# One shared SBUF arena and one PSUM block against many separate tiles, in a state-space and long-convolution kernel

## The chip, the core and the metric

The kernel runs on one NeuronCore of a Trainium2 chip. The core has five engines with an instruction queue each: TensorE (PE, matmuls; PEld are its weight loads), VectorE (DVE), ScalarE (ACT), GpSimd (POOL) and SyncE (SP, which here only issues DMAs). Each queue runs strictly in its written order; engines wait for one another, and for DMAs, through semaphores. The metric is device time in microseconds (us) of one execution.

## What is computed

Two sequence mixers read the same `x` (2048 steps, 1024 channels) and are blended by a gate of one number per step. Cut to what matters:

```python
x = A_x
g = sigmoid((x * gate_w).sum(-1, keepdims=True))
# a: complex diagonal state space model, 1024 states
h = Lam_bar[None, :] * h + Bu[:, t, :]          # for each of the 2048 steps
y = 2.0 * einsum("blp,dp->bld", hseq, Cmat).real + x * Dskip
# b: 4-tap shift convolution of k, times v, then a 2048-long convolution per channel by FFT
kv = k_shift * v
y = irfft(rfft(kv_pad) * rfft(kf_pad))[:S] + kv * ssm_D
b = x * y
return g * a + (1 - g) * b
```

## The kernel before

**Two halves in one program.** The convolution `b` is done in 8 units of 128 channels (`for u in range(NU)`). A unit loads `k` and `v` transposed (L522, L523, DMA transposes on SP), makes the short convolution by matmuls (L558) and multiplies by `v` (DVE, L561), stores the product to DRAM (L568, POOL) and loads it back in another layout together with the filter (L573, POOL, one load each). Then come the matrix form of the FFT: `stage1` (matmul L589; its results are copied from PSUM into the place `z`), `spec` (matmuls L602 to L604, copied into `kv`), `product` (DVE, L614 to L617, into `pp`), `inverse` (matmuls L628 to L630, copied into `qq`), and four DMAs of 64 KB from `qq` into `zb` (L635, on SP; 4 for each of 4 quarters of a unit, 128 in all). `zb` is laid out by partitions, and each of these DMAs writes every sixteenth partition, beginning with partition `k2`. `final` (matmuls L648, L649) reads `zb`, and its result goes to DRAM (L652).

The state space half `a` goes by 4 blocks of 512 steps. For each of 8 groups of states, `rot_ops` makes a rotation table (DVE L709 to L711 in F32 in the places `wt1` and `wt2`, then ACT L714 and L305), `in_ops` multiplies (matmul L742), rotates (DVE L752 to L754), scans (L757) and rotates back (L766 to L768). `c_ops` prepares the output matrices (L799, L803), and `out_ops` multiplies by them (matmuls L825, L831), gates (ACT L835), adds (DVE L837) and stores (L838). The first block's groups are interleaved with the 8 convolution units; the second, third and fourth blocks fill what is left and the end.

**Copies out of PSUM** all go through one helper, `evac`: ACT does it on L426, DVE on L424, whichever a planner chose. 172 of the 1024-column copies are ACT's, 36 are DVE's.

**What sets the order.** `Planner` lists every operation, gives each buffer a place by number and each operation an engine and a slot, and the program is written out in that order; a chain of order-only edges at the end keeps every engine's instructions in it. `places` gives the permitted numbers for each kind of buffer, in KB of a partition for SBUF ("S") and in banks for PSUM ("P"): `z` lies at 80 to 95, `zb` at 96 to 103 or 188 to 195, `wt1` at 164 and 165, `wt2` at 166 and 167, `qq` at 120 and 121 or 122 and 123. `view` turns a place into an address: in this kernel a slice of one SBUF tile `arena` or of one PSUM tile `banks`. The semaphore waits are put in afterwards by the recording layer, which compares each instruction's accesses with earlier accesses to the same tile.

Of the kernel before, what the change touches and what calls it, by code (L numbers as in the profile page):

```python
# [11 lines left out]
BF16 = mybir.dt.bfloat16  # L12
F32 = mybir.dt.float32
# [162 lines left out]
def kernel(  # L176
# [25 lines left out]
    S, D = xf.shape  # L202
# [17 lines left out]
    consts = ctx.enter_context(tc.tile_pool(name="consts", bufs=1))  # L220
    dram = ctx.enter_context(tc.tile_pool(name="dramscr", bufs=1, space=bass.MemoryType.DRAM))
    parm = ctx.enter_context(tc.tile_pool(name="parm", bufs=1))
    psum = ctx.enter_context(tc.tile_pool(name="psum", bufs=1, space=bass.MemoryType.PSUM))
    pB_scr = dram.tile([S, D], BF16, name="pB_scr")
    kv_scr = dram.tile([D, S], BF16, name="kv_scr")
    pB_v = pB_scr.rearrange("(j g) d -> j g d", g=16)
    AR_KB = 201
    arena = consts.tile([128, AR_KB * 512], BF16, name="arena")
    banks = psum.tile([128, 8, 512], F32, name="banks")


    def at(first, n, step, *guards):
        return [(first + step * i, guards) for i in range(n)]
# [7 lines left out]
    if 1 == 2:  # L241
# [18 lines left out]
        "ot": ("S", 2, free2 + extra),  # L260
        "ps": ("P", 2, at(0, 4, 2)), "bu": ("P", 2, at(6, 1, 0) + at(0, 3, 2)), "psy": ("P", 2, at(0, 4, 2)),
    }
    pl = Planner(places)
    pl.limit = {"ps": 4, "bu": 2, "psy": 3, "x": 4, "pb": 4, "ga": 3, "ot": 4, "cs": 8}
    op = pl.op

    def view(t):
        mem, size, _ = places[t.tag]
        dims = t.shape[1:]
        n = math.prod(dims)  # L270
        if mem == "P":
            flat = banks[:, t.off:t.off + size, :].rearrange("p a b -> p (a b)")
            if t.dt is BF16:
                flat = flat.bitcast(BF16)
            flat = flat[:, 0:n]
        elif t.dt is F32:
            flat = arena[:, t.off * 512:t.off * 512 + 2 * n].bitcast(F32)
        else:
            flat = arena[:, t.off * 512:t.off * 512 + n]
        if len(dims) == 1:  # L280
            return flat
        names = "abcdef"[:len(dims)]
        return flat.rearrange(f"p ({' '.join(names)}) -> p {' '.join(names)}", **dict(zip(names, dims)))

    T.look = staticmethod(view)
    PE, ACTE, DVE, POOL = "PE", "ACT", "DVE", "POOL"
    MM = {512: 0.216, 256: 0.112, 128: 0.064}
# [296 lines left out]
    def stage1(a, z, w, q):  # L584
        ps = tile_("ps", [128, 4, 256], F32)

        def f(e):
            for i in range(4):
                nc.tensor.matmul(ps.ap[:, i, :], lhsT=a.ap[:, 4 * q + i, :], rhs=tabS.ap[:, 0:256], start=True, stop=True)  # L589
        o = op({PE: 4 * MM[256]}, f, [a, rT1], [ps, z])  # L590
        evac(lambda: z.ap[:, :, w, :, 32 * q:32 * q + 32].rearrange("p k r (g c) -> p k r g c", c=8),
             lambda: ps.ap.rearrange("p g (k r c) -> p k r g c", r=2, c=8), [ps], [z], 1.05)
        return o
# [48 lines left out]
    def final(zb, u, h):  # L642
        ps, cv = tile_("ps", [128, 2, 4, CH], F32), tile_("cv", [128, 8, CH])

        def f(e):
            for i in range(2):
                g0 = 8 * h + 4 * i
                nc.tensor.matmul(ps.ap[:, i], lhsT=tabS.ap[:, 256:384], rhs=zb.ap[:, g0:g0 + 4, 0, :], start=True, stop=False)  # L648
                nc.tensor.matmul(ps.ap[:, i], lhsT=tabS.ap[:, 384:512], rhs=zb.ap[:, g0:g0 + 4, 1, :], start=False, stop=True)  # L649
        o = op({PE: 4 * MM[512]}, f, [zb, rT2], [ps, cv])  # L650
        evac(lambda: cv.ap, lambda: ps.ap.rearrange("p a g c -> p (a g) c"), [ps], [cv])
        op(dma("POOL", 256), lambda e: nc.gpsimd.dma_start(  # L652
            out=pB_v[:, 8 * h:8 * h + 8, u * CH:(u + 1) * CH], in_=cv.ap), [cv], [convd])
        return o

    for u in range(NU):
# [8 lines left out]
        for q in range(4):  # L665
            pl.key = base + 0.5 * q - 4.0
            o = stage1(kas[u], zz[u], 0, q)
# [17 lines left out]
        for h in range(2):  # L685
            o = final(zb, u, h)
# [221 lines left out]
```

## Time and profile before

| | |
|---|---|
| time before, median of 2 runs | 595.6 us (593.55 to 597.65) |
| the profiled execution's own time | 594.96 us |
| its span, first to last instruction | 593.2 us |
| PE busy | 432.5 us, 73% |
| DVE busy | 383.4 us, 65% |
| ACT busy | 290.0 us, 49% |
| POOL busy | 62.1 us, 10% |

The share of busy time is a mean over very different stretches, so the table by stretches and the lists of waits say more. "Granted clock" is the share of TensorE's full speed (2.4 GHz; the lower of its two levels is 1.2 GHz) that the records show. Idle time before an instruction stands in square brackets in a timeline, with what ended it; "issue" there means that no releaser was found. "SPq" is a DMA issue on SP's queue.

### The profile page before, as it was taken

How to read it: one execution, taken by the hardware profiler on the slowest of the kernel's cores; microseconds unless marked ns; L12 is line 12 of the kernel's file. 1: busy time of each engine (PE TensorE's matmuls, PEld its weight loads, DVE VectorE, ACT ScalarE, POOL GpSimd, SP SyncE). 2: the span in 40 equal slices, each digit the busy share in tenths (PEclk: the TensorE clock that was granted, in tenths of full speed). 3: DMA queues.
4: the chain of work that ended last, by engine and by line, in shares of the span. 5: the costliest groups of instructions: out<-in, count | busy, mean ns of one | idle time of the engine just before them, and what ended most of it. 6: DMA issues, size and time to landing. Idle time of an engine off the chain costs nothing. (4 is left out here: it accounts for less than half of the span.)

```text
span 593.2 us, 6880 instructions
## 1 busy us (share of the span) xinstructions
PE 432.5 (73%) x2529; PEld 235.2 (40%) x2529; DVE 383.4 (65%) x573; ACT 290.0 (49%) x364; POOL 62.1 (10%) x102
## 2 busy tenths in 40 slices
PE   2527755945836765914764684796999999999996
PEld 1424333532524442512342352452444445444443
DVE  6567680933834645602657381698999999998950
ACT  5685424733734545512644562697895223322111
POOL 3210010100010010102011010000211102000000
PEclk9778785987977787875896796798999999999999
DMA  7899583462731732466242331375852446100100
GB/s 132 184 191 207 123 134 73 117 111 53 152 88 40 142 94 63 88 130 146 62 134 65 69 88 36 71 148 119 184 137 71 143 90 179 52 19 18 38 35 36
DMA packets 118026, 60.25 MB, mean 102 GB/s; under 512 B 93416, under 2 KB 109800, under 8 KB 117992
## 3 DMA queue, kind: packets, MB, share of 16 engines
q1 hardware_dynamic: 109576, 34.62, 29.9%
q0 software_dynamic: 7296, 25.17, 16.2%
q8 instruction: 20, 0.33, 0.2%
q10 hardware_dynamic: 1120, 0.02, 0.1%
q14 instruction: 14, 0.11, 0.1%
HBM read 16.80 MB, written 12.58 MB: 50 GB/s over the span
## 5 line engine op out<-in xcount | busy, mean ns | idle before, releaser
L426 ACT CAST arena<-banks 128x1024 bf16<-128x1024 f32 x172 | 165.9, 1019 | 190.7 <-DMA arena<-arena 100.9
L742 PE MATMUL banks<-arena 128*128 128x512 bf16 x512 | 124.0, 394 | 9.9 <-ACT arena L426 5.8
L825 PE MATMUL banks<-arena 128*128 128x512 bf16 x512 | 117.4, 381 | 1.3 <-DVE arena L803 1.1
L589 PE MATMUL banks<-arena 128*128 128x256 bf16 x256 | 43.1, 324 | 60.3 <-ACT arena L426 57.2
L742 PEld LDWEIGHTS <-arena 128*128 128x128 bf16 x512 | 51.4, 101 | 69.8 <-issue 17.8
L825 PEld LDWEIGHTS <-arena 128*128 128x128 bf16 x512 | 49.5, 98 | 59.2 <-issue 2.5
L602 PE MATMUL banks<-arena 128*128 128x512 bf16 x128 | 53.3, 416 | 24.9 <-ACT arena L426 17.3
L424 DVE CAST arena<-banks 128x1024 bf16<-128x1024 f32 x36 | 43.4, 1220 | 28.8 <-DMA arena<-arena 17.2
L589 PEld LDWEIGHTS <-arena 128*128 128x128 bf16 x256 | 28.7, 113 | 71.9 <-issue 64.2
L628 PE MATMUL banks<-arena 128*128 128x256 bf16 x128 | 33.4, 293 | 19.7 <-DVE arena L424 9.0
L835 ACT ACTIVATE arena<-banks,gcols 128x1024 bf16<-128x1024 f32 x16 | 17.5, 1113 | 46.1 <-PE banks L825 46.0
L558 PE MATMUL banks<-arena 128*128 128x512 bf16 (+1 forms) x112 | 34.4, 468 | 7.5 <-DMA arena<-in_B_k_dram 3.3
L614 DVE TENSOR_TENSOR arena<-arena 128x1024 bf16<-128x1024 bf16 x32 | 21.9, 684 | 26.3 <-ACT arena L426 26.2
L603 PE MATMUL banks<-arena 128*128 128x256 bf16 x128 | 37.5, 293 | 0.0
L604 PE MATMUL banks<-arena 128*128 128x256 bf16 x128 | 37.4, 292 | 0.0
L652 POOL DMA_DIRECT2D pB_scr<-arena x16 | 14.3, 893 | 163.8 <-ACT arena L426 156.6
L630 PE MATMUL banks<-arena 128*128 128x128 bf16 x128 | 29.9, 233 | 0.0
L629 PE MATMUL banks<-arena 128*128 128x128 bf16 x128 | 29.9, 233 | 0.0
L752 DVE TENSOR_TENSOR arena<-arena 128x1024 bf16<-128x1024 bf16 x32 | 21.9, 685 | 11.3 <-ACT arena L305 10.8
L648 PE MATMUL banks<-arena 128*128 128x512 bf16 x32 | 13.0, 407 | 18.3 <-ACT arena L426 6.6
L837 DVE TENSOR_TENSOR arena<-arena 128x1024 bf16<-128x1024 bf16 x16 | 11.0, 688 | 22.9 <-ACT arena L835 22.8
L709 DVE TENSOR_SCALAR arena<-iota_row,thn 128x512 f32<-128x512 f32 x8 | 3.9, 485 | 33.5 <-DMA arena<-arena 19.8
(162 smaller groups left out, 631.1 us busy)
## 6 DMA issues: line engine op xcount, KB each, us to landing
arena<-arena SPq DMA_DIRECT2D x128, 64.0 KB
arena<-in_B_ssm_k_dram POOLq DMA_DIRECT2D x8, 512.0 KB, 6.0
kv_scr<-arena POOLq DMA_DIRECT2D x8, 512.0 KB, 4.4
arena<-kv_scr POOLq DMA_DIRECT2D x8, 512.0 KB, 6.0
pB_scr<-arena POOLq DMA_DIRECT2D x16, 256.0 KB, 3.6
arena<-in_A_x_dram POOLq DMA_DIRECT2D x16, 256.0 KB, 3.5
arena<-pB_scr POOLq DMA_DIRECT2D x16, 256.0 KB, 4.0
out_dram<-arena SPq DMA_DIRECT2D x16, 256.0 KB
```

The source lines that it names most:

```text
L424: nc.vector.tensor_copy(o(), i_())
L426: nc.scalar.copy(o(), i_())
L558: nc.tensor.matmul(ps.ap[:, i, lo:512], lhsT=dg.ap[:, s_, :], rhs=kT.ap[:, t0 + lo - s_:t0 + 512 - s_], start=(s_ == 0), stop=(s_ == KS - 1))
L589: nc.tensor.matmul(ps.ap[:, i, :], lhsT=a.ap[:, 4 * q + i, :], rhs=tabS.ap[:, 0:256], start=True, stop=True)
L602: nc.tensor.matmul(o, lhsT=tabF.ap[:, 0, k2, :], rhs=x, start=True, stop=False)
L603: nc.tensor.matmul(o[:, :, 0, :], lhsT=tabF.ap[:, 1, k2, :], rhs=x[:, :, 1, :], start=False, stop=False)
L604: nc.tensor.matmul(o[:, :, 1, :], lhsT=tabF.ap[:, 2, k2, :], rhs=x[:, :, 0, :], start=False, stop=True)
L628: nc.tensor.matmul(o, lhsT=tabG.ap[:, 0, k2, :], rhs=x, start=True, stop=False)
L629: nc.tensor.matmul(o[:, 0, :], lhsT=tabG.ap[:, 2, k2, :], rhs=x[:, 1, :], start=False, stop=False)
L630: nc.tensor.matmul(o[:, 1, :], lhsT=tabG.ap[:, 1, k2, :], rhs=x[:, 0, :], start=False, stop=True)
L742: nc.tensor.matmul(ps.ap[:, r, :], lhsT=BT[dt_][r].ap[:, pi * 128:(pi + 1) * 128], rhs=xT.ap[:, dt_, :], start=(dt_ == 0), stop=(dt_ == ND ...
L825: nc.tensor.matmul(psy.ap[:, dh, :], lhsT=hbs[(tb, pi)].ap[:, r, tl * 128:(tl + 1) * 128], rhs=CT[pi][r].ap[:, dh * 512:(dh + 1) * 512], s ...
```

## The change

`arena` is replaced by a list of tiles: the SBUF places of all kinds of buffers are sorted, those that overlap are joined into a span, and every span gets a tile of its own (57 of them, `ar0`, `ar1`, ...). `z` and each place of `zb`, `qq`, `wt1`, `wt2`, `kv` and so on thereby lie in tiles of their own. `banks` becomes four tiles of two banks each. `view` looks up the tile of a place. Shapes, types and the planner's tables are as they were. Line numbers behind the new lines are 9 higher.

```diff
-    AR_KB = 201
-    arena = consts.tile([128, AR_KB * 512], BF16, name="arena")
-    banks = psum.tile([128, 8, 512], F32, name="banks")
+    banks = [psum.tile([128, 1024], F32, name=f"bank{i}") for i in range(4)]
...
+    spans = []
+    for a, b in sorted((o, o + size) for m, size, offs in places.values() if m == "S" for o, _ in offs):
+        if spans and a < spans[-1][1]:
+            spans[-1][1] = max(b, spans[-1][1])
+        else:
+            spans.append([a, b])
+    home = {}
+    for i, (a, b) in enumerate(spans):
+        t = consts.tile([128, (b - a) * 512], BF16, name=f"ar{i}")
+        for k in range(a, b):
+            home[k] = (t, a)
...
         if mem == "P":
-            flat = banks[:, t.off:t.off + size, :].rearrange("p a b -> p (a b)")
+            flat = banks[t.off // 2]
             if t.dt is BF16:
                 flat = flat.bitcast(BF16)
             flat = flat[:, 0:n]
-        elif t.dt is F32:
-            flat = arena[:, t.off * 512:t.off * 512 + 2 * n].bitcast(F32)
         else:
-            flat = arena[:, t.off * 512:t.off * 512 + n]
+            a, a0 = home[t.off]
+            a0 = (t.off - a0) * 512
+            flat = a[:, a0:a0 + 2 * n].bitcast(F32) if t.dt is F32 else a[:, a0:a0 + n]
```

In the built programs each engine has the same instructions in the same order before and after; what differs is what they wait for. In the rows below a wait is named by its semaphore: `DMAHW0` to `DMAHW7` are those of SP's DMAs, `DMASW` those of POOL's, the others those of an engine.

ScalarE, third convolution unit, where `stage1`'s results (128x16x2x32, into `z`) and two `qq` copies are written and the rotation table's L714 follows; before:

```order
L426 CAST arena<-banks 128x16x2x32 [waits DMAHW3_49,DMAHW5_49,DMAHW2_49,DMAHW6_49,DMAHW1_49,DMAHW7_49,DMAHW0_49,PE_49]
L426 CAST arena<-banks 128x16x2x32 [waits PE_49]
L426 CAST arena<-banks 128x1024 [waits PE_49,Activation_49]
L426 CAST arena<-banks 128x16x2x32 [waits PE_49]
L426 CAST arena<-banks 128x16x2x32 [waits DMAHW3_49,DMAHW2_49,PE_49]
L426 CAST arena<-banks 128x1024
L426 CAST arena<-banks 128x1024 [waits PE_49,Activation_49]
L426 CAST arena<-banks 128x16x2x32 [waits DMAHW4_49,DMAHW5_49,DVE_49,PE_49]
L714 ACTIVATE arena<-arena 128x512 [waits DMAHW7_49,DMAHW6_49,DVE_49]
```

and now:

```order
L435 CAST ar_98<-bank_68 128x16x2x32 [waits PE_49]
L435 CAST ar_98<-bank_71 128x16x2x32 [waits PE_49]
L435 CAST ar_106<-bank_70 128x1024 [waits DMAHW1_49,DMAHW2_49,DMAHW0_49,DMAHW3_49,PE_49,Activation_49]
L435 CAST ar_98<-bank_68 128x16x2x32 [waits PE_49]
L435 CAST ar_98<-bank_71 128x16x2x32 [waits PE_49]
L435 CAST ar_117<-bank_69 128x1024
L435 CAST ar_107<-bank_68 128x1024 [waits DMAHW5_49,DMAHW6_49,DMAHW0_49,DMAHW7_49,PE_49,Activation_49]
L435 CAST ar_98<-bank_70 128x16x2x32 [waits DVE_49,PE_49]
L723 ACTIVATE ar_120<-ar_119 128x512 [waits DVE_49]
```

The `z` copies and L714 (now L723) no longer wait for SP's DMAs; the two copies into `qq` (`ar_106`, `ar_107`) do, for the DMAs that last read these places.

VectorE at the same place, the rotation table's three steps between `z` copies; before:

```order
L709 TENSOR_SCALAR arena<-iota_row,thn 128x512 [waits DMAHW4_49,DMAHW5_49,DMAHW3_49,DMAHW6_49,DMAHW2_49,DMAHW7_49,DMAHW1_49,DMAHW0_49]
L424 CAST arena<-banks 128x16x2x32 [waits PE_49,Activation_49]
L710 TENSOR_SCALAR arena<-arena 128x512 [waits DMAHW5_49,DMAHW4_49,DVE_49]
L424 CAST arena<-banks 128x16x2x32 [waits PE_49,Activation_49]
L711 TENSOR_TENSOR arena<-arena 128x512 [waits DMAHW6_49,DVE_49]
L424 CAST arena<-banks 128x16x2x32 [waits DMAHW7_49,PE_49,Activation_49]
```

and now:

```order
L718 TENSOR_SCALAR ar_119<-iota_row,thn 128x512
L433 CAST ar_98<-bank_70 128x16x2x32 [waits PE_49,Activation_49]
L719 TENSOR_SCALAR ar_120<-ar_119 128x512 [waits DVE_49]
L433 CAST ar_98<-bank_71 128x16x2x32 [waits PE_49,Activation_49]
L720 TENSOR_TENSOR ar_119<-ar_119,ar_120 128x512 [waits DVE_49]
L433 CAST ar_98<-bank_69 128x16x2x32 [waits PE_49,Activation_49]
```

All waits for SP's DMAs are gone from them.

SyncE at the same place, the eight DMAs of the unit's last two quarters; before:

```order
L635 DMA arena<-arena 8x16x256 [waits DMAHW2_49,Activation_49]
L635 DMA arena<-arena 8x16x256 [waits DMAHW3_49]
L635 DMA arena<-arena 8x16x256 [waits DMAHW4_49,DVE_49,Activation_49]
L635 DMA arena<-arena 8x16x256 [waits DMAHW5_49]
L635 DMA arena<-arena 8x16x256 [waits DMAHW6_49,DVE_49,Activation_49]
L635 DMA arena<-arena 8x16x256 [waits DMAHW7_49,DVE_49]
L635 DMA arena<-arena 8x16x256 [waits DMAHW0_49,DVE_49,Activation_49]
L635 DMA arena<-arena 8x16x256 [waits DMAHW1_49]
```

and now:

```order
L644 DMA ar_125<-ar_106 8x16x256 [waits DMAHW2_49,Activation_49]
L644 DMA ar_125<-ar_106 8x16x256 [waits DMAHW3_49]
L644 DMA ar_125<-ar_106 8x16x256 [waits DMAHW4_49]
L644 DMA ar_125<-ar_106 8x16x256 [waits DMAHW5_49]
L644 DMA ar_125<-ar_107 8x16x256 [waits DMAHW6_49,Activation_49]
L644 DMA ar_125<-ar_107 8x16x256 [waits DMAHW7_49]
L644 DMA ar_125<-ar_107 8x16x256 [waits DMAHW0_49]
L644 DMA ar_125<-ar_107 8x16x256 [waits DMAHW1_49]
```

Each group of four now waits once for an engine, for the copy that fills its `qq` place; the `DMAHW` wait of each row is that for the DMA issued eight before it and stays.

## Rows read from the trace of the kernel before

**Rows 1.** Stretches: start:end, length; busy us (instructions) of PE, PEld, DVE, ACT, POOL; granted clock; DMA share; GB/s.
```profile
17.00:69.00 52.00, 27.55 (x212) 18.23 (x210) 32.83 (x47) 32.62 (x54) 8.16 (x23) 0.79 1.04 195
69.00:120.00 51.00, 37.72 (x220) 21.90 (x219) 31.82 (x48) 25.86 (x35) 5.22 (x6) 0.81 0.51 100
120.00:165.00 45.00, 28.28 (x186) 17.32 (x185) 22.39 (x35) 22.51 (x29) 4.67 (x5) 0.85 0.53 103
165.00:210.00 45.00, 27.62 (x160) 16.34 (x159) 22.51 (x34) 20.50 (x27) 3.77 (x4) 0.77 0.43 92
210.00:252.00 42.00, 29.32 (x170) 16.85 (x169) 23.09 (x36) 21.57 (x29) 5.28 (x6) 0.80 0.36 81
252.00:308.00 56.00, 29.30 (x202) 17.52 (x200) 22.34 (x34) 21.52 (x27) 7.47 (x10) 0.76 0.51 118
308.00:351.00 43.00, 27.90 (x170) 17.14 (x170) 26.11 (x47) 24.17 (x29) 3.22 (x3) 0.80 0.29 68
351.00:405.00 54.00, 39.01 (x252) 22.75 (x250) 36.01 (x54) 35.29 (x40) 2.67 (x3) 0.84 0.44 93
405.00:440.00 35.00, 31.36 (x166) 14.39 (x167) 31.37 (x43) 30.04 (x35) 7.16 (x12) 0.95 0.75 166
440.00:593.00 153.00, 148.15 (x791) 70.41 (x789) 123.61 (x175) 45.90 (x53) 9.62 (x18) 1.00 0.22 68
```

**Rows 2.** Line L635, who waited for its DMAs: us in total, times (ACT's two rows).
```profile
  ACT arena L426: 100.9, 21
...
  ACT arena L714: 26.8, 4
```

**Rows 3.** The DMA queue's own waits on SP: waiter, releaser, us, times, longest us.
```profile
SPq L635 <- ACT arena L426: 82.6, 24, 7.1
```

**Rows 4.** ScalarE's timeline, 119 to 146 us: start us, us, engine, line, operation [idle before].
```profile
122.15 3.76 ACT L426 CAST arena<-banks 128x1024 bf16<-128x1024 f32 x4 [2.71 <-DMA arena<-arena]
132.44 2.84 ACT L426 CAST arena<-banks 128x1024 bf16<-128x1024 f32 x3 [6.52 <-DMA arena<-arena]
137.50 1.01 ACT L426 CAST arena<-banks 128x1024 bf16<-128x1024 f32 x1 [2.22 <-DMA arena<-arena]
145.86 0.63 ACT L714 ACTIVATE arena<-arena 128x512 f32<-128x512 f32 x1 [7.35 <-DMA arena<-arena]
```

**Rows 5.** VectorE's timeline in the same stretch.
```profile
132.61 0.49 DVE L709 TENSOR_SCALAR arena<-iota_row,thn 128x512 f32<-128x512 f32 x1 [10.21 <-issue]
...
137.53 0.43 DVE L710 TENSOR_SCALAR arena<-arena 128x512 f32<-128x512 f32 x1 [3.29 <-DMA arena<-arena]
...
142.68 0.69 DVE L711 TENSOR_TENSOR arena<-arena 128x512 f32<-128x512 f32 x1 [3.59 <-DMA arena<-arena]
145.88 1.22 DVE L424 CAST arena<-banks 128x1024 bf16<-128x1024 f32 x1 [2.50 <-DMA arena<-arena]
147.02 2.35 DVE L561 TENSOR_TENSOR arena<-banks,arena 128x1024 bf16<-128x1024 f32 x2
```

**Rows 6.** SyncE's timeline, 110 to 150 us (xN merges N issues with the waits between).
```profile
110.47 2.52 SPq L635 DMA_DIRECT2D arena<-arena  x4
...
125.94 23.47 SPq L635 DMA_DIRECT2D arena<-arena  x8
```

**Rows 7.** TensorE's timeline in the same stretch, the rows before which it was idle.
```profile
123.22 0.60 PE L589 MATMUL banks<-arena 128*128 128x256 bf16 x4 [1.72 <-ACT arena L426]
...
133.50 2.72 PE L589 MATMUL banks<-arena 128*128 128x256 bf16 x12 [6.20 <-ACT arena L426]
...
139.14 1.89 PE L558 MATMUL banks<-arena 128*128 128x512 bf16 x8 [1.10 <-DVE arena L424]
147.16 0.61 PE L602 MATMUL banks<-arena 128*128 128x512 bf16 x1 [6.13 <-DVE arena L424]
```

**Rows 8.** The program's waits over the whole span: waiter, releaser, us in total, times, longest us.
```profile
PE banks L589 <- ACT arena L426: 57.2, 14, 13.1
```

**Rows 9.** DMA issues: destination, source, count, KB each, median us to landing.
```profile
arena<-in_B_ssm_k_dram POOLq DMA_DIRECT2D x8, 512.0 KB, 6.0
```

## What the change will do: the prediction, made before it ran

> **What bounds the kernel now.** I read the page first, then a table by stretches cut at the starts of `stage1`, then the waits for line L635, then one unit instruction by instruction. The stretches fall into two kinds [rows 1]. From 440 us to the end PE is busy 148.15 of 153.00 us at a granted clock of 1.00: that part is PE's own and has nothing to give. From 69 to 405 us, seven convolution units long, PE is busy in only 219.2 of 336 us (37.72 + 28.28 + 27.62 + 29.32 + 29.30 + 27.90 + 39.01), DVE in 184 and ACT in 171, and the clock is 0.76 to 0.85. No engine bounds this part; they wait for each other. The list of those who waited for the `qq` to `zb` DMAs of L635 says for what: ACT alone stood 100.9 us before copies on L426 and 26.8 us before L714, 127.7 us in 25 waits [rows 2]. These instructions write `z` and read `wt1`. Neither shares a byte with `qq` or `zb`: the places are 80 to 95 and 164 to 167 against 120 to 123, 96 to 103 and 188 to 195. So the waits are for nothing; the recording layer takes two accesses to different parts of one tile for overlapping.
>
> One unit shows how they lock. From 119.44 us (122.15 less the 2.71 of idle) to 146 ACT waits four times for these DMAs: 2.71 + 6.52 + 2.22 + 7.35 = 18.8 us [rows 4]. DVE waits four times: 10.21 + 3.29 + 3.59 + 2.50 = 19.6 us [rows 5]; the first of these, put down to "issue", is the one with eight DMA semaphores in the order shown above. And SP, which has eight DMAs to issue, takes 23.47 us over them [rows 6], where four took 2.52 us before, because each pair in its turn waits for the copy that ACT or DVE has just made. Over the program SP waits 82.6 us for ACT's L426 in this way [rows 3]. It is a game of ping-pong: a pair of DMAs lands, one copy runs, the next pair is let go.
>
> **The change, part by part.** By the built programs no instruction moves, and none is added but wait instructions are dropped. Three things change in the waits.
>
> (1) 27 instructions of ACT and 20 of DVE lose their waits for L635, and 33 issues of SP lose waits for ACT or DVE. What is left in the unit above? ACT's stretch from 119.44 to 146.49 is 27.0 us; without its 18.8 us of waits it has 8.2 us of work. DVE's, from 122.4 to 147.02, is 24.6 us; without 19.6 it has 5.0. PE's, from 121.5 to 147.16, is 25.7 us, and it was idle 1.72 + 6.20 + 1.10 + 6.13 = 15.2 us in it [rows 7], each time for a copy of ACT or DVE that a DMA held. Without them it has 10.5 us. PE is the longest of the three, so the stretch shrinks from about 25.7 to 10.5 us and this unit from 45 to 29.8 us, of which PE is then busy in 28.28: a share of 0.95.
>
> So PE becomes the bound of the units, and the sum must not be ACT's 127.7 us: 336 less 127.7 is 208 us, less than PE's 219.2 us of work. I go by PE's share instead. The trace shows 0.90 in the stretch 405 to 440, where DVE (31.37 of 35) and ACT (30.04) are just as full and no such wait occurs, and 0.97 from 440 on [rows 1]. Between them I take 0.93: 219.2 / 0.93 = 235.7 us in place of 336, **a gain of 100 us**. Bounds: PE at a share of 1.00 gains 117; and as the other end only what PE itself stood idle behind ACT at `stage1`, 57.2 us [rows 8].
>
> The first stretch, 17 to 69 us, I count at nothing: its DMA share is 1.04 [rows 1], it is fed by the loads, and these don't change. The last, from 405 on, also nothing: PE is busy there in 179.5 of 188 us.
>
> (2) 23 copies into `qq` (19 of ACT, 4 of DVE) get a wait for the four DMAs that last read that place. This was true before too, but an earlier wait of the same engine covered it. Behind such a copy stand all later copies of ACT, and PE behind them. I cost it at nothing: in the unit shown the copy that runs as the third of the four from 122.15 would wait for DMAs issued from 110.47 to 112.99 [rows 4, 6]. Even at the longest wait for these DMAs in that unit, 7.35 us [rows 4], they have landed by 120.4. If the cover goes, because SP runs late, the price is up to 7.35 us each.
>
> (3) PSUM: PE's waits are the same by the built programs. Nothing.
>
> What is late next: `final` reads `zb`, so the last four DMAs of a unit must land before L648; they leave SP earlier now, at the pace of 2.52 us for four. And the filter load for the next unit can only be issued when `stage1` has read the old one; it takes 6.0 us to land [rows 9], and `stage1` comes again a unit later, about 30 us. Both have cover.
>
> The sum: the profiled execution's span of 593.2 less 100 is 493; with the 1.8 us around the span (594.96 less 593.2) 495. The median of the runs is 595.6, 0.6 above the profiled execution, which is within their spread. A denser PE should also be granted more clock than the 0.76 to 0.85 of the units, and so do the same matmuls in less time. From 0.80 to 0.88 would take some 20 us off the 219 (estimate, by the ratio); I count 1 us of it in the value, and 10 in the lower bound: **494 us**.
>
> **The page that speaks against it.** The waits measured here are 127.7 us in 25, or 5.1 us each [rows 2]. The Trainium skill's page "SBUF — State Buffer", section "The DMA setup-cost knee", gives a transfer about 2 us plus its bytes at 436 GB/s, which makes 2.15 us for 64 KB, an estimate from that page. By it 25 waits would be worth 54 us and the time would be some 541 us. The rows disagree, since what is waited for is a group of DMAs behind others, and I go by the rows.
>
> **The rivals.**
>
> *Only part of it.* The copies start earlier, but other order in the units holds PE: a quarter's chain of matmul, copy, product, matmul, copy. Then only PE's idle behind ACT at `stage1` goes, 57.2 us [rows 8]: 538 us. For it: the engines' queues are fixed, and PE waits at other places too (6.13 us at L602 above). Against: this idle too stood behind a held copy. The page's price above would end at nearly the same time.
>
> *The DMAs crowd.* The DMA work of the seven units is 149 us by share times length (26.0 + 23.9 + 19.4 + 15.1 + 28.6 + 12.5 + 23.8) [rows 1]. In 236 us that is a share of 0.63, where 0.44 was. If each unit's last group then lands in 7.35 us and not the 2.22 that the shortest wait shows [rows 4], PE waits 5.1 us more at L648 in each of seven units, 36 us: 530 us. The Trainium skill's "DMA: Bandwidth & Descriptors", section "Issuing engines are not separate DMA queues", says that the DMAs of SP, ACT and POOL all run on the same 16 engines and interleave, so that POOL's loads would slow these. The stretch at 1.04 is the only one where the rows show them full.
>
> *Slower.* The new waits of (2) become the lock that the old ones were: with SP behind by a DMA's landing at every quarter, each of the 23 copies stops its engine. It breaks even where each costs 100 / 23 = 4.4 us, and is 2% slower (12 us) from 4.9 us on; at the longest wait seen, 7.35 us, it would be 23 x 7.35 = 169 us lost against 100 won, 664 us. Against it: two `qq` places stand by turns, and the margin was 9 us above.
>
> *No change.* The releasers of the profile are inferred; if the DMAs' waits only stood beside others that end as late, the time stays at 595. Against it: the remaining waits in the order are for PE, which was itself waiting.
>
> **How the numbers follow.** The likeliest, PE bound with all false waits gone, 475 to 515 us: 0.70. More than that, by the clock: 0.08. Part of it or crowded DMAs, 515 to 560: 0.15. No change: 0.03. Slower: 0.04. A measurement of this kernel can tell about 2% from no change, so faster is 0.93, within 2% 0.03, slower 0.04. The range goes from PE at a share of 1.00 with 10 us of clock (595 - 117 - 10 = 468) to the 57.2 us end, cut to 535; about 0.05 lies below it and 0.15 above.
>
> **What would show it.** Right: ACT's and DVE's waits for L635 vanish from the list of waits; SP's eight issues of a unit's second half take a few us more than two groups of 2.5; the units are 28 to 34 us long with PE busy nine tenths; the last 150 us are the same. Step (2) is wrong if copies of L435 or L433 into `qq` wait for these DMAs for more than a few us. Crowding shows as PE idle at L657 (now `final`) with a DMA as releaser. The forecast is wrong if the units stay over 40 us, or if PE's idle time goes to a load of POOL that I counted as covered.

## The result, and the profile after

The changed kernel takes 494.3 us (median of 2 runs, 492.83 to 495.78) against 595.6: a ratio of 0.830, 95% interval 0.814 to 0.846. The forecast was 494, with a range of 468 to 535. The number is nearly exact, and partly by luck: it hides two terms that were each wrong by some 25 us and cancelled. The lock itself was read rightly.

The profiled execution's span is 494.0 us, 99.2 less than before. Here are the stretches of after, cut near the starts of `stage1` as [rows 1] is (start:end, length; busy us and instructions of PE, PEld, DVE, ACT, POOL; granted clock; DMA share; GB/s):

```profile
17.00:69.00 52.00, 30.94 (x226) 21.44 (x228) 34.59 (x49) 34.38 (x56) 8.15 (x23) 0.77 1.02 193
69.00:110.00 41.00, 32.24 (x191) 18.62 (x193) 28.30 (x43) 22.87 (x32) 4.72 (x6) 0.88 0.67 125
110.00:140.00 30.00, 26.44 (x187) 16.78 (x188) 23.46 (x39) 23.59 (x32) 4.84 (x6) 1.00 0.77 157
140.00:167.00 27.00, 23.23 (x167) 15.05 (x169) 23.40 (x35) 20.57 (x29) 4.10 (x5) 1.00 0.76 156
167.00:197.00 30.00, 25.61 (x165) 15.37 (x165) 22.68 (x36) 21.16 (x28) 5.18 (x6) 0.89 0.50 113
197.00:236.00 39.00, 27.78 (x210) 17.68 (x212) 25.10 (x39) 22.16 (x29) 7.60 (x10) 0.87 0.89 164
236.00:263.00 27.00, 22.64 (x161) 14.30 (x161) 23.30 (x43) 23.43 (x28) 3.23 (x4) 1.00 0.61 118
263.00:306.00 43.00, 36.44 (x246) 21.74 (x247) 35.83 (x54) 34.95 (x40) 2.67 (x3) 0.92 0.68 116
...
341.00:494.00 153.00, 147.08 (x775) 70.31 (x788) 123.36 (x174) 45.61 (x52) 9.62 (x18) 0.99 0.23 68
```

The seven units from 69 to 306 us are 237 us long where they were 336: the 99 us are all there. The last 153 us are the same in both kernels. Two columns differ from what the prediction built on. PE's busy time in these units is 194 us and not 219, at a clock of 0.87 to 1.00 and not 0.76 to 0.85; and PE's share is 194.4 of 237, 0.82, not 0.93. (The profile lacks 42 of this run's 2529 matmul records, 19 of them in these stretches; at about 0.2 us each they would make the share 0.84.)

The list of those who wait for the `qq` to `zb` DMAs (now L644; us in total, times):

```profile
  PEld L657: 17.9, 4
  PE bank_71 L657: 12.8, 3
  DVE ar_107 L433: 11.2, 1
  PE bank_68 L657: 10.6, 4
  PE bank_69 L657: 4.3, 1
```

ACT is gone from it, where it had 127.7 us [rows 2]. What is left is `final` (now L657), which truly reads `zb`, and one copy into `qq`. PE's idle behind ACT at `stage1`, 57.2 us before [rows 8], is some 4 us now. The stretch that [rows 4] to [rows 7] showed, in the timelines of ACT, DVE, SP and PE after (start us, us, engine, line, operation, count, idle before in brackets):

```profile
112.00 1.01 ACT L435 CAST ar_98<-bank_68 128x1024 bf16<-128x1024 f32 x1 [0.78 <-PE bank_68 L598]
...
118.64 1.05 ACT L435 CAST ar_98<-bank_70 128x1024 bf16<-128x1024 f32 x1
119.75 0.63 ACT L723 ACTIVATE ar_120<-ar_119 128x512 f32<-128x512 f32 x1
```
```profile
114.11 0.48 DVE L718 TENSOR_SCALAR ar_119<-iota_row,thn 128x512 f32<-128x512 f32 x1
116.43 1.23 DVE L433 CAST ar_98<-bank_70 128x1024 bf16<-128x1024 f32 x1 [1.84 <-PE bank_70 L598]
...
120.80 1.23 DVE L570 TENSOR_TENSOR ar_113<-bank_68,ar_112 128x1024 bf16<-128x1024 f32 x1
```
```profile
114.87 3.12 SPq L644 DMA_DIRECT2D ar_125<-ar_106  x4
118.79 2.52 SPq L644 DMA_DIRECT2D ar_125<-ar_107  x4
```
```profile
127.44 0.38 PE L657 MATMUL bank_68<-ar_125,ar_128 128*128 128x512 bf16 x1 [3.27 <-DMA ar_125<-ar_107]
```

From the first `z` copy to L723, ACT now takes 7.8 us; from the first to L714 it took 23.7 [rows 4]. SP's eight DMAs take 6.4 us, not 23.5 [rows 6]. But look at the last line: SP's last issue ends at 121.31, and `final` starts only at 127.44, 6.1 us later, after 3.27 us of idle PE.

### The profile page after: what moved, and what is told of

It is laid out like the page before. It is cut to its first block, busy times and chain, and to the rows that moved or that the text cites. A ratio compares the mean times of both kernels' runs of the same rounds, so it can differ in the third digit from the quotient of the medians.

```text
span 494.0 us, 6786 instructions
## 1 busy us (share of the span) xinstructions
PE 410.0 (83%) x2487; PEld 228.1 (46%) x2529; DVE 382.7 (77%) x573; ACT 288.8 (58%) x364; POOL 62.2 (13%) x102
## 4 chain that ended last, share of the span: by engine, by line
PE 58%; DMA 15%; ACT 10%; SPq 9%; DVE 5%; issue 2%; DVEq 0%; ACTq 0%
PE bank_71 L834 7%; PE bank_69 L834 7%; DMA ar_99<-ar_107 6%; PE bank_70 L751 5%; PE bank_69 L751 5%; PE bank_68 L751 5%; DMA ar_125<-ar_107 4%; SPq L644 4%; PE bank_71 L751 3%; ACT ar_98 L435 3%; PE bank_70 L834 3%; DMA ar_112<-in_B_v_dram 3%; SPq L711 2%; PE bank_68 L834 2%; DMA ar_116<-in_A_x_dram 2%
## 5 line engine op out<-in xcount | busy, mean ns | idle before, releaser
L661 POOL DMA_DIRECT2D pB_scr<-ar_108 x16 | 14.3, 893 | 136.4 <-ACT ar_108 L435 129.2
L763 DVE TENSOR_TENSOR ar_121<-ar_119,ar_120 128x1024 bf16<-128x1024 bf16 x32 | 22.1, 692 | 1.1
L623 DVE TENSOR_TENSOR ar_102<-ar_100 128x1024 bf16<-128x1024 bf16 x16 | 11.0, 684 | 15.4 <-ACT ar_100 L435 15.4
L611 PE MATMUL bank_70<-ar_98,ar_96 128*128 128x512 bf16 x36 | 14.1, 392 | 9.8 <-DVE ar_107 L433 9.6
L567 PEld LDWEIGHTS <-ar_115 128*128 128x128 bf16 x112 | 12.3, 110 | 19.6 <-issue 7.3
L613 PEld LDWEIGHTS <-ar_96 128*128 128x128 bf16 x128 | 13.1, 103 | 17.0 <-issue 3.3
L834 PEld LDWEIGHTS <-ar_123 128*128 128x128 bf16 x128 | 12.5, 98 | 15.1
L612 PEld LDWEIGHTS <-ar_96 128*128 128x128 bf16 x128 | 13.0, 102 | 13.9 <-issue 10.9
L766 DVE TENSOR_TENSOR_SCAN ar_122<-rv,ar_121 128x512 bf16<-128x512 f32 x16 | 19.0, 1213 | 0.0
L611 PEld LDWEIGHTS <-ar_96 128*128 128x128 bf16 x128 | 13.0, 102 | 12.5 <-DVE ar_98 L433 9.5
L657 PEld LDWEIGHTS <-ar_128 128*128 128x128 bf16 x32 | 3.3, 103 | 33.2 <-issue 27.9
L834 PEld LDWEIGHTS <-ar_124 128*128 128x128 bf16 x128 | 12.2, 98 | 13.2
L435 ACT CAST ar_101<-bank_70 128x1024 bf16<-128x1024 f32 x11 | 11.4, 1036 | 11.0 <-PE bank_70 L613 10.4
L611 PE MATMUL bank_68<-ar_98,ar_96 128*128 128x512 bf16 x22 | 8.6, 389 | 10.1 <-ACT ar_98 L435 10.1
L638 PEld LDWEIGHTS <-ar_97 128*128 128x128 bf16 x128 | 12.9, 101 | 7.9 <-issue 5.9
L567 PE MATMUL bank_69<-ar_111,ar_115 128*128 128x512 bf16 (+3 forms) x46 | 12.9, 423 | 3.4 <-DMA ar_111<-in_B_k_dram 3.3
L771 ACT CAST WL<-ar_122 128x2 f32<-128x2 bf16 x24 | 4.9, 204 | 18.4 <-DVE ar_122 L766 18.4
L435 ACT CAST ar_117<-bank_70 128x1024 bf16<-128x1024 f32 x4 | 4.0, 1012 | 19.5 <-PE bank_70 L751 12.8
L598 PEld LDWEIGHTS <-ar_110 128*128 128x128 bf16 x128 | 12.5, 99 | 6.3 <-issue 4.3
L435 ACT CAST ar_108<-bank_71 128x1024 bf16<-128x1024 f32 x7 | 7.1, 1016 | 13.9 <-PE bank_71 L658 13.6
L435 ACT CAST ar_98<-bank_71 128x1024 bf16<-128x1024 f32 x14 | 14.6, 1044 | 0.2 <-PE bank_71 L598 0.2
L637 PEld LDWEIGHTS <-ar_97 128*128 128x128 bf16 x128 | 12.9, 101 | 2.9 <-DVE ar_105 L626 0.7
```

Source lines behind the costliest of these rows:

```text
L435: nc.scalar.copy(o(), i_())
L567: nc.tensor.matmul(ps.ap[:, i, lo:512], lhsT=dg.ap[:, s_, :], rhs=kT.ap[:, t0 + lo - s_:t0 + 512 - s_], start=(s_ == 0), stop=(s_ == KS - 1))
L611: nc.tensor.matmul(o, lhsT=tabF.ap[:, 0, k2, :], rhs=x, start=True, stop=False)
L612: nc.tensor.matmul(o[:, :, 0, :], lhsT=tabF.ap[:, 1, k2, :], rhs=x[:, :, 1, :], start=False, stop=False)
L613: nc.tensor.matmul(o[:, :, 1, :], lhsT=tabF.ap[:, 2, k2, :], rhs=x[:, :, 0, :], start=False, stop=True)
L637: nc.tensor.matmul(o, lhsT=tabG.ap[:, 0, k2, :], rhs=x, start=True, stop=False)
```

## The experiments

All are compared with runs of the kernel before on the same chip. Line numbers move with each edit; the stages are named.

### Which part of the change does it

Two kernels do one part of it each.

```diff
# psum_own: the kernel before, with only this
-    banks = psum.tile([128, 8, 512], F32, name="banks")
+    banks = [psum.tile([128, 1024], F32, name=f"bank{i}") for i in range(4)]
...
-            flat = banks[:, t.off:t.off + size, :].rearrange("p a b -> p (a b)")
+            flat = banks[t.off // 2]
```

> One part alone: PSUM in four tiles, SBUF still one arena. Theory (the time hangs on the waits alone): every instruction waits for the same instructions as in the kernel before, so 595 us, ratio 1.00 within 0.01. Rival (the PSUM tiles take part in the gain): at least 10 us less, 585 or below.

Measured: 596.9 us, ratio 1.003 (0.999 to 1.007). The PSUM tiles alone change nothing.

```diff
# zb_own: the changed kernel, with only some spans given tiles of their own
+    own = (96, 188)
+    shared = consts.tile([128, sum(b - a for a, b in spans if a not in own) * 512], BF16, name="arena")
...
-        t = consts.tile([128, (b - a) * 512], BF16, name=f"ar{i}")
+        if a in own:
+            t, a0 = consts.tile([128, (b - a) * 512], BF16, name=f"ar{i}"), a
+        else:
+            t, a0 = shared, a - at_
+            at_ += b - a
...
```

> One part alone: of all SBUF places only zb's two get tiles of their own, all others lie in one shared tile (PSUM in four tiles). Theory (false overlap of the L635 DMAs' writes into zb with other places of the same tile is the whole cause): every instruction waits for the same instructions as in the changed kernel, so 494 us, ratio 0.83 within 0.01. Rival (the many separate tiles, or the new addresses, matter too): 505 us or more.

Measured: 490.8 us, ratio 0.825 (0.817 to 0.833), which is the changed kernel's within both intervals. So 55 of the 57 tiles do nothing. Two places had to leave the arena, those into which the L635 DMAs write. So all the false waits that cost time were between these DMAs and other places of the same tile. That they come from the writes to every sixteenth partition is not shown: no run changed the stride, and why the recording layer takes such a write that way was not looked into.

### Do the waits add up?

The same edit with `own = (80,)`, that is `z` alone, and with `own = (164, 166)`, `wt1` and `wt2` alone.

> Only z gets a tile of its own: the copies into z lose their waits for the L635 DMAs, the rotation table's steps (L709 to L711, L714) keep theirs. Theory A (the waits add up by ACT's share): 100.9 of ACT's 127.7 us go, 100.9/127.7 of 101 us = 80 us won, 515 us. Theory B (a serial lock: in each of the seven units DVE's three or four steps, 76 us in all by the trace of before, still each wait for a pair of DMAs): 494 + 56 to 76, 550 to 570 us.

> The complement: only wt1 and wt2 get tiles of their own, the copies into z keep their waits. Theory A (the waits add up by ACT's share): 26.8/127.7 of 101 us = 21 us won, 574 us. Theory B (serial lock: two to four copies of each unit still wait for a pair each, though the rotation steps between them are free): 565 to 585 us, and the gains of this run and of its complement together stay under the 101 us of the whole.

Measured: `z_own` 543.2 us, ratio 0.915 (0.907 to 0.923), a gain of 52 us; `wt_own` 571.6 us, ratio 0.960 (0.952 to 0.968), a gain of 23. Together 75 us, against 104 for `zb_own` on the same chip. The waits for these DMAs that remain, first in `z_own`, then in `wt_own` (ACT and DVE, us in total, times, longest):

```profile
ACT arena L730 <- DMA arena<-arena: 29.8, 4, 11.5
...
DVE arena L725 <- DMA arena<-arena: 25.1, 4, 13.8
DVE arena L727 <- DMA arena<-arena: 20.6, 5, 5.9
DVE arena L726 <- DMA arena<-arena: 13.3, 4, 4.6
```
```profile
ACT arena L442 <- DMA arena<-arena: 105.0, 23, 13.4
...
DVE arena L440 <- DMA arena<-arena: 70.9, 11, 10.6
```

With `z` free, ACT's idle for these DMAs falls from 127.7 us [rows 2] to 29.8, by 98, and the time by 52. With the table's places free, the waits of L709 to L711 and L714 are gone, 102.8 us by the list of L635's waiters (30.0 + 26.1 + 19.9 + 26.8, only the last row shown), and the `z` copies on DVE wait 71 us where they had waited 17.2. Theory A, shares that add, is out by 28 us for `z_own`, and theory B's window is missed too, by 7 us at its fast end; for `wt_own` the two theories were too close to tell apart. The sum of both gains, under the whole, speaks for a lock as in B, if a looser one: half a lock still locks, and idle time that leaves one line comes back on the next.

### What bounds the units now: PE, or the way through zb?

In the changed kernel `final` waits for `zb`, and the four L644 of the last quarter take longer to land than before. Two suspects were made lighter in turn. The order on PE, DVE, ACT and SP stays.

```diff
# light_kv: the transposing loads of k and v, ahead of the zb DMAs on SP
-        ... nc.sync.dma_start_transpose(out=kT.ap, in_=kf[:, c0:c0 + 128]) ...
+        ... nc.sync.dma_start_transpose(
+            out=kT.ap if u == 0 else kT.ap[:, 0:128], in_=kf[:, c0:c0 + 128] if u == 0 else kf[0:128, c0:c0 + 128]) ...
```

> The changed kernel with the transposing loads of k and v cut to a sixteenth of their bytes in units 1 to 7 (128 of 2048 steps are loaded, the rest is what the unit before left), so that the output is not the reference's; order and waits stay. Theory (crowding: the zb DMAs land late because they share rings and engines with the transposes before them on SP): the time from a unit's last zb issue to final falls from some 6 us towards the 2.5 of the kernel before, PE's idle at final from 23 us to under 8, the time to 475 to 482. Rival (this is what such DMAs cost when four follow each other): idle at final stays at 18 or more, time 488 or more.

Measured: 476.9 us, ratio 0.807 (0.801 to 0.812). The time is in the window that the theory gave, and the theory is wrong: the landing did not shrink. SP's timeline, PE's and that of its weight loads at the same unit (107 to 114 us here):

```profile
101.56 6.44 SPq L646 DMA_DIRECT2D ar<-ar  x8
```
```profile
113.96 0.38 PE L659 MATMUL bank<-ar,ar 128*128 128x512 bf16 x1 [3.10 <-DVE ar L627]
```
```profile
113.93 0.10 PEld L659 LDWEIGHTS <-ar 128*128 128x128 bf16 x1 [3.35 <-DMA ar<-ar]
```

From the last issue's end at 108.00 to `final` is 6.0 us, as before the edit. The row of `final` itself names DVE, but its weight load, 0.03 us earlier, had waited for these DMAs. For the last groups of the eight units in turn, this time is 5.3, 6.1, 5.6, 6.3, 4.1, 4.1, 5.0 and 2.4 us in the changed kernel, and 5.2, 6.0, 5.7, 6.2, 4.5, 4.2, 4.7 and 2.5 here. PE's idle time before `final`, whatever releaser the profile names, fell only from 27.7 to 20.3 us, and nearly all of that at the first group (from 8.4 to 1.6). By the idle time the rival (18 or more) is right, by the total time it is not. Where the time went is said below, by stretches.

```diff
# light_pool: POOL's loads of the filter and of kv_scr
-            out=t.ap, in_=src[u * CH:(u + 1) * CH, :].rearrange("(g c) (n m) -> (c n) g m", c=8, m=128)), r, [t])
+            out=t.ap if u == 0 else t.ap[:, 0:1], in_=src[u * CH:u * CH + (CH if u == 0 else 8), :].rearrange(
+                "(g c) (n m) -> (c n) g m", c=8, m=128)), r, [t])
```

> The changed kernel with POOL's two loads of a unit (the filter and the product read back, 512 KB each) cut to a sixteenth in units 1 to 7, the rest being what the unit before left, so that the output is not the reference's. The lighter k and v loads did not shorten the landing of the zb DMAs (5 to 6 us), so it is not the transposes; in the trace 4096-byte packets of POOL's queue run among theirs. Theory (POOL's transfers crowd them): the time from a unit's last zb issue to final falls to 2.5 to 4 us, the waits of final from some 50 us (its weight loads, all releasers) to under 30, time 475 to 486. Rival (eight DMAs one after another simply take that long): 5 to 6 us to final as before, time 489 or more.

Measured: 459.7 us, ratio 0.772 (0.762 to 0.781): more than expected, and of the expected kind. SP and PE at the same unit:

```profile
100.75 6.44 SPq L645 DMA_DIRECT2D ar<-ar  x8
```
```profile
109.89 0.38 PE L658 MATMUL bank<-ar,ar 128*128 128x512 bf16 x1
```

2.7 us from the last issue's end at 107.19 to `final`, and PE does not wait. For the eight groups in turn it is 4.2, 2.7, 3.0, 2.5, 3.0, 3.2, 4.1 and 2.4 us, and PE's idle time before `final` is 8.1 us in all. That the two loads themselves came late is no rival: in the changed kernel's lists PE and its weight loads wait for neither. But not all of the landing is theirs: at the seventh group no such load is under way, two transposing loads of SP (of `Cmat`) follow the group, and PE waits 4.0 us in the changed kernel and 3.6 here. Last, PE itself was given less to do.

```diff
# light_pe: spec with one matmul of three
-                nc.tensor.matmul(o, lhsT=tabF.ap[:, 0, k2, :], rhs=x, start=True, stop=False)
-                nc.tensor.matmul(o[:, :, 0, :], lhsT=tabF.ap[:, 1, k2, :], rhs=x[:, :, 1, :], start=False, stop=False)
-                nc.tensor.matmul(o[:, :, 1, :], lhsT=tabF.ap[:, 2, k2, :], rhs=x[:, :, 0, :], start=False, stop=True)
+                nc.tensor.matmul(o, lhsT=tabF.ap[:, 0, k2, :], rhs=x, start=True, stop=True)
```

> The changed kernel with two of the three matmuls of each spec step left out (those of the imaginary tables), so that the output is not the reference's: 16 x 2 x 0.108 = 3.4 us of PE work less in each of eight units, 28 us in all; every other instruction and wait as it was. Theory of the prediction (PE is the bound of the units): 24 to 30 us less, 465 to 472. Rival (the units are bound by a loop through PE, the PSUM copies, SP's issues and the landing in zb, PE being only a part of it): 5 to 16 us less, 479 to 490, and PE's busy share in the units falls under 0.8.

Measured: 485.2 us, ratio 0.817 (0.810 to 0.825). Against 0.825 to 0.830 for kernels with the same waits that is 4 to 8 us for 28 us of work taken away, at or under the low end of the rival's window, and with intervals that overlap it may be less; the 24 us of the first theory can be excluded. PE's idle time before `final` rose from 27.7 to 31.8 us, and its share in the six units of the table below is 138.04 of 180.00, 0.77, under 0.8 as the rival has it. PE alone is not what bounds the units of the changed kernel.

The stretches say it best: unit 1 first, then the six units from the next `stage1` to the first output matmul. In order: the changed kernel, `zb_own` (the same waits), `light_kv`, `light_pool`, `light_pe` (columns as above).

```profile
66.00:111.00 45.00, 36.19 (x215) 20.99 (x218) 32.26 (x49) 25.72 (x36) 5.53 (x7) 0.89 0.67 127
111.00:294.00 183.00, 151.25 (x1053) 95.37 (x1069) 140.88 (x222) 132.86 (x167) 27.13 (x30) 0.93 0.70 136
```
```profile
66.00:107.00 41.00, 35.72 (x213) 20.62 (x215) 31.82 (x48) 25.85 (x35) 5.23 (x6) 0.92 0.73 139
107.00:291.00 184.00, 152.99 (x1052) 96.91 (x1068) 140.76 (x222) 132.89 (x165) 27.18 (x30) 0.93 0.68 136
```
```profile
63.00:98.00 35.00, 33.01 (x213) 19.72 (x216) 31.86 (x48) 25.68 (x35) 5.23 (x6) 1.00 0.49 122
98.00:278.00 180.00, 149.83 (x1056) 94.97 (x1071) 140.86 (x222) 132.97 (x165) 27.18 (x30) 0.95 0.59 120
```
```profile
63.00:97.00 34.00, 33.00 (x213) 19.70 (x216) 31.84 (x49) 25.57 (x35) 4.00 (x6) 1.00 0.58 123
97.00:260.00 163.00, 148.24 (x1052) 95.64 (x1068) 139.30 (x222) 132.11 (x166) 21.05 (x30) 0.96 0.60 122
```
```profile
62.00:105.00 43.00, 31.96 (x181) 17.27 (x181) 31.38 (x46) 24.32 (x34) 4.33 (x5) 0.88 0.80 139
105.00:285.00 180.00, 138.04 (x868) 78.19 (x881) 141.00 (x225) 132.99 (x167) 28.09 (x31) 0.90 0.70 139
```

Either load made lighter takes 10 or 11 us off unit 1; 4 of them lie within what kernels with the same waits differ by, since `zb_own` has 41.00 there. In the changed kernel's chain of waits two pieces show it (start us, us, what):

```profile
75.33 15.14 DMA ar_112<-in_B_v_dram
...
90.50 5.73 DMA ar_99<-ar_107
```

The load of `v` is 15 us under way, and the last `zb` DMA of the unit is issued only when it has landed. Of the six later units `light_kv` takes 3 us, `light_pool` 20, `light_pe` 3. So of what was made lighter it is POOL's two loads that hold these units most, and with them small PE is busy in 148.24 of 163 us, a share of 0.91, near the 0.93 that the prediction had assumed. What `light_pe` took away in these units was 6 x 3.4 = 20.7 us; PE's busy time fell by 13 only; its clock fell from 0.93 to 0.90 with it, which by the ratio accounts for some 4 of the 7 us between (an estimate).

### Can the landing be covered instead?

If the loads can't be spared, PE could do other work before `final`. Three kernels let the planner lay a new order: with a longer landing of the `zb` DMAs in its model (3.0 and 5.0 us in place of 1.6), and with a later due time of `final`.

```diff
# lat3, lat5: 3.0 or 5.0
-                o.end = self.dma[e] + 1.6
+                o.end = self.dma[e] + max(1.6, o.lat)
...
-                in_=qq.ap[:, i].rearrange("p r c -> p (r c)")), [qq], [zb])
+                in_=qq.ap[:, i].rearrange("p r c -> p (r c)")), [qq], [zb], lat=5.0)
# fin13
-        pl.key = base + 2.0 + 0.9 * 21.94
+        pl.key = base + 2.0 + 1.3 * 21.94
```

> The changed kernel planned with 3.0 us instead of 1.6 from a zb DMA's transfer to its landing, so the planner puts other PE work ahead of final in most units. Theory (final simply comes too early in PE's queue): PE's idle at final falls from 23 to 8 to 14 us, time 478 to 486. Rival (the units are bound by the chain of copy, issue, landing itself): the idle goes to other lines, time 490 or more.

> The same with 5.0 us. Theory: PE's idle at final under 10 us, time 475 to 485. Rival: as above, or slower, since final's result is stored and the zb places come free later: 490 to 505.

> The changed kernel with the planner's due time of final 0.4 of a unit later (1.3 in place of 0.9). Theory (final too early): idle at final 23 to under 12, time 480 to 487. Rival: no gain, 490 to 500, because units are bound by the chain through zb.

Measured: `lat3` 485.8 us, ratio 0.818 (0.813 to 0.823); `lat5` 481.7, 0.810 (0.805 to 0.816); `fin13` 482.0, 0.813 (0.809 to 0.817). `lat5` is the fastest kernel that does the whole computation, though its interval overlaps that of `fin13`. It lies just beside that of `zb_own` (0.817 to 0.833) and overlaps that of the changed kernel (0.814 to 0.846), so the gain is some 2% and not clear of noise in each comparison. PE's idle time before `final` is 11.3, 7.2 and 16.0 us in the three, 27.7 in the changed kernel; `fin13` has the time that was expected, and not the idle time (under 12). In `lat5` the list of PE's waits shows where part of it went (waiter, releaser, us, times, longest):

```profile
PE bank L637 <- DVE ar L626: 13.0, 5, 5.6
...
PE bank L611 <- DVE ar L433: 11.3, 3, 10.3
```

`inverse` (L637) now waits for DVE's product, 13.0 us where it was 2.4 in the changed kernel. Since the planner laid a new order, these three also differ in more than the place of `final`.

## Why the prediction was right, point by point

**The lock.** Right, and shown. The waits of ACT and DVE for L635 are gone, SP's eight issues take 6.4 us in the unit shown, and giving `zb` alone tiles of its own gives the whole gain.

**The sum must not be ACT's 127.7 us.** Right. `z_own` shows it from the other side: 98 us of ACT's waits less, 52 us of time.

**PE's work, 219.2 us.** Wrong by about 20 to 25 us. The prediction saw that a denser PE would be granted more clock, put it at some 20 us, and then counted 1 of it. Measured: 194.4 us (some 198 with the missing records) at 0.87 to 1.00. The Trainium skill's "TensorE: Matmul & The Clock Gate", section "What's actually happening", describes TensorE's clock as going by its recent activity; the rows agree in direction, 0.76 to 0.85 with the stalls and 0.87 to 1.00 without, and `light_pe`, with less PE work, fell to 0.90.

**PE's share, 0.93.** Wrong for this kernel: 0.82 (0.84). It was taken from stretches without the false waits, and that alone was not enough: the 405 to 440 stretch has no `stage1` loads. With POOL's loads made lighter the share is 0.91. The two errors cancel, and that is luck: 219.2 / 0.93 = 235.7 us forecast, 194.4 / 0.82 = 237 measured. The prediction's own signs were met only in part. It wanted units of 28 to 34 us with PE busy nine tenths, and called itself wrong if they stay over 40: the seven are 41, 30, 27, 30, 39, 27 and 43 us long.

**The rival "the DMAs crowd"** was priced at 36 us and given part of 0.15, as an alternative. It is true, beside the likeliest case: PE waits 23.4 us at `final` in the seven units (8.4 + 7.3 + 4.4 + 3.3 in the list of PE's waits; the 4.3 there are of the eighth), and `light_pool` is 31 us faster than `zb_own` and 35 faster than the changed kernel. The price was of the right size and the place was right; that the clock would pay for it was not seen. These waits, by releaser:

```profile
PE bank_71 L657 <- DMA ar_99<-ar_107: 8.4, 1, 8.4
...
PE bank_68 L657 <- DMA ar_99<-ar_107: 7.3, 3, 4.0
PE bank_71 L657 <- DMA ar_125<-ar_107: 4.4, 2, 3.6
PE bank_69 L657 <- DMA ar_125<-ar_107: 4.3, 1, 4.3
...
PE bank_68 L657 <- DMA ar_125<-ar_107: 3.3, 1, 3.3
```

**"What is late next" had said that `final` is covered.** Wrong, and this is the step that failed: it looked at how early the DMAs leave SP, not at what else would be on the DMA engines when they land. The Trainium skill's "DMA: Bandwidth & Descriptors", section "Issuing engines are not separate DMA queues", says that transfers from all queues interleave on the same engines. `light_pool` agrees: 2.7 us instead of 6.1 from the last issue to `final`, with only POOL's transfers made smaller. In the kernel before, the false waits had kept the two apart: in the unit of [rows 6] POOL's two loads were issued at 126.5 and 136.5 us and the last `zb` issue ended at 149.4, where they are now issued at 116.4 and 119.1 and it ends at 121.3.

**The new waits of the `qq` copies, counted at nothing.** Right for 22 of 23, by the list of those who wait. One, in the fifth of these units, cost DVE 11.17 us and PE 9.6 behind it:

```profile
215.65 1.23 DVE L433 CAST ar_107<-bank_70 128x1024 bf16<-128x1024 f32 x1 [11.17 <-DMA ar_99<-ar_107]
```
```profile
193.85 6.90 SPq L711 DMA_TRANSPOSE ar_116<-in_A_x_dram  x5
200.85 4.92 SPq L532 DMA_TRANSPOSE ar_112<-in_B_v_dram  x1
205.85 2.54 SPq L644 DMA_DIRECT2D ar_99<-ar_107  x4
```

SP issues five transposes of `x` and one of `v` before the four DMAs that free this place; of the seven units this is the one in whose midst the next block's `xT` is loaded. That is the mechanism of the rival "slower", at one place out of 23.

**The ends and PSUM.** Right: the last 153 us are the same, the first stretch hardly moved, `psum_own` is 1.003.

**The page's price of 2.15 us for a 64 KB transfer** (the Trainium skill's "SBUF — State Buffer", section "The DMA setup-cost knee") would have made 541 us. By the measured gain a wait was worth 99.2 / 25 = 4.0 us. That it cost a transfer behind others and the loop through the next copy, and not one transfer, is a reading of the timelines that no run tested.

## What to carry to other kernels

Look in the list of waits for instructions that wait on a DMA whose bytes they don't touch; here such waits came from the tracking of one tile shared by many buffers, and it was enough to move the two places into which the DMAs write. When a lock goes, don't subtract its waits: bound the stretch by the busiest engine, at the clock that it will then be granted, and ask which transfers will now fall on each other. A total that comes out right is no proof of its terms; look at busy time and share apart.

## What the runs showed of the hardware

Taking 20.7 us of matmuls out of six units lowered PE's busy time by only 13 us and its granted clock from 0.93 to 0.90. In the unit shown, `final` finds the `zb` DMAs, 64 KB each in groups of four, landed 2.7 us after the last issue with POOL's loads small, and waits for them until 6.1 us after it with these loads at full size, while cutting the transposing loads of `k` and `v` on their own queue to a sixteenth changed nothing in that (6.0 us).
